# Convolution and two MLPs on one core: scaling by bank, another order of the first units, and two unused matmuls

## The chip, the cores and the metric

The kernel runs on one core of a Trainium2 chip. The time is that of the device for one execution in microseconds (us), the median of several runs. The core's engines are TensorE (PE, matmul), VectorE (DVE), ScalarE (ACT), GpSimd (POOL) and SyncE (SP, which issues the transfers here). They run side by side and wait for each other through semaphores.

## What is computed

8192 tokens of 192 features go through three steps in float32. The first is a causal convolution: each token sums itself and its six predecessors, with seven weights for each of 8 heads of 24 features, which are a softmax of `weight_gen`. The second is a gated MLP on the normalized rows, the third a plain one.

```python
w = np.exp(weight_gen - max); w = w / (sum(w) + 1e-9)      # 7 taps, 8 heads
x = einsum('bshk,bskhg->bshg', w, x_unf)                    # 8192 x 192
xn = x / np.sqrt(np.mean(x * x, -1) + 1e-6) * rms_g
g, val = xn @ w_gate, xn @ w_val                            # 192 x 1536
x = (g * sigmoid(g) * val) @ w_out                          # 1536 x 192
h = x @ w_in                                                # 192 x 2048
out = (h * sigmoid(1.702 * h)) @ w_out2                     # 2048 x 192
```

## The kernel before

The tokens go in 16 blocks of 512, four tiles of 128 each. A partition holds a run of 64 consecutive tokens. For a block the convolution is done with tokens on the partitions; then each row is scaled by its root mean square, the block is transposed on PE (`transpose_x`, L352), and it is split into a high part (`xh`, `xsh`, by ACT, L362) and a low part (`xl`, `xsl`, by DVE, L364), since a float32 product is made of three faster matmuls: high by high, low by high, high by low. `xh` and `xl` hold features 0 to 127, `xsh` and `xsl` the other 64 twice. So the copies of the scaling on ACT (L288) write features 128 to 191 a second time.

The blocks 0 and 1 are special. Block 0's taps are summed by DVE in two PSUM banks `ac` and `bc`, two tiles each: products into `xr` (L229), additions onto the banks (L256). Block 1's products are made by GpSimd and summed by PE through the identity (L247). ACT makes the square sums (L273), GpSimd the root: a multiply-add and a power (L278, L280). The result `ri` scales the rows.

The work of the MLPs is cut into units. A unit of the first MLP (`U1(b, m)`, 12 to a block) is the matmuls of one 128-wide piece of gate and value into two PSUM banks `pg` and `pv` (L381), then ACT's silu to `p` (L486), DVE's product (`second`, L490), ACT's cast to the high part `h` (L491) and DVE's subtraction to the low part `l` (`third`, L494). The matmuls with the down weights (`D1`, into the banks `a` and `b`) run two units later, within that unit's matmuls. There are four banks for `pg` and `pv`, so those of unit n are used again by unit n + 2. Every matmul uses half of the array's rows (64), two run side by side, and `matmuls` writes the two sequences as pairs; a bank goes from upper to lower rows through a GpSimd word (L396). A unit of the second MLP (`U2`) is alike, with two silu (L507, L508) and one subtraction for each half (L514).

The weights arrive as 64-bit words in 34 pieces, three at a time, and are turned into high and low parts on the way: ACT makes a first value (`x1`, L95), DVE cuts signs and masks (`x2`, L99 and L103), merges (`x3`, L107), cuts the high part (`x4`, L111), makes the low part (`x5`, L117), and ACT casts the high part (`x6`, L122). Pieces are called `w` (for `U1` and `U2`) and `o` (for `D1` and `D2`). While the pieces come in, in the first 120 us, they share DVE and ACT with the units of blocks 0 and 1.

The order on every engine is that of the program (`manual_schedule`). The list `units` sets the order of the units; `need` says at which unit each piece is due; `piece_steps` interleaves the steps of three pieces; `add_work`, `share` and `some` spread this and the later blocks' convolutions over the units, by costs in ns written in the code. The units before begin 0_0, 0_1, 1_0, 0_2, 1_1, 0_3, 1_2, 0_4, 0_5, 1_3, 0_6 (block and m), by this line:

```python
units += [(1, 0, t) for t in range(len([u for u in units if u[1] == 0]), min(M1, m + LAG + m // 3 + 1))]
units += [(1, 1, m)]
```

The softmax of blocks 2 and 3 needs one exponential on ACT (`ex_hook`, L188), placed four units after the start of that block's work; ACT loads a table before it and another one after it.

Of the kernel before, what the change touches and what calls it, by code (L numbers as in the profile page):

```python
# [9 lines left out]
F32 = mybir.dt.float32  # L10
F32R = mybir.dt.float32r
# [3 lines left out]
ALU = mybir.AluOpType  # L15
# [15 lines left out]
BLOCKS = [4] * 16  # L31
GROUPS = [(0, 1), (1, 2), (2, 4), (4, 7), (7, 10), (10, 13), (13, 16)]
AHEAD = 4
LAG = 1
LAG2 = 3
NST = 3
LOOK = 1
# [5 lines left out]
def gated_conv_mlp(ctx: ExitStack, tc: tile.TileContext, xp, wg, w1, wo1, w2, wo2, g, out):  # L43
# [113 lines left out]
    def softmax_load(gi):  # L157
        b0, b1 = GROUPS[gi]
        n = sum(BLOCKS[b0:b1])
        t = smw.tile([P, n * 56], F32, tag="wraw", name=f"wraw{gi}")  # L160
        nc.sync.dma_start(out=t, in_=wg[:, T0[b0] * 56:(T0[b0] + n) * 56])
        return t
# [55 lines left out]
    def conv_ops(b):  # L218

        T = BLOCKS[b]  # L220
        Q = T * HEADS
        x = xch[b]
        wn = wn_of[b]
        xr = att.tile([P, T, 2 * P], F32, tag="xr", name=f"xr{b}")
        prod = xr.rearrange("p t c -> p (t c)")[:, 0:Q * GRP]
        ops = []

        def mul(eng, k, dst, j0=0, j1=T):
            eng.tensor_tensor(  # L229
                out=dst.rearrange("p (q g) -> p q g", g=GRP),  # L230
                in0=x[:, (k + j0) * D:(k + j1) * D].rearrange("p (q g) -> p q g", g=GRP),
                in1=wn[:, j0 * HEADS:j1 * HEADS, k:k + 1].to_broadcast([P, (j1 - j0) * HEADS, GRP]), op=ALU.mult)
        cost = 1.04 * Q * GRP + 70
        if b < 2:
            S = T // 2
            sums_of = [pacc.tile([P, NM], F32, tag=f"{n}{b}", name=f"{n}c_{b}") for n in "ab"]
            acc_of = [sums_of[j // S][:, (j % S) * D:(j % S + 1) * D] for j in range(T)]
        else:
            acc = att.tile([P, T, D], F32, tag="acc", name=f"acc{b}")
            acc_of = [acc[:, j] for j in range(T)]  # L240
        if b == 1:
            def tap(k):
                for i, ps in enumerate(sums_of):
                    tag = (("yh", "yl"), ("ysh", "ysl"), ("yh0", "yl0"))[k % 3][i]
                    pr = ytp.tile([P, NM], F32R, tag=tag, name=f"pr{k}_{i}").bitcast(F32)[:, :S * D]
                    mul(nc.gpsimd, k, pr, i * S, (i + 1) * S)
                    nc.tensor.matmul(ps[:, :S * D], ident, pr, start=k == 0, stop=k == TAPS - 1)  # L247
            ops += [(cost, lambda k=k: tap(k)) for k in range(TAPS)]
        elif b == 0:
            n = S * D  # L250

            def tap(k):
                for i, ps in enumerate(sums_of):
                    mul(nc.vector, k, prod[:, i * n:(i + 1) * n] if k else ps[:, :n], i * S, (i + 1) * S)
                for i, ps in enumerate(sums_of if k else ()):
                    nc.vector.tensor_tensor(out=ps[:, :n], in0=ps[:, :n], in1=prod[:, i * n:(i + 1) * n], op=ALU.add)  # L256
            ops += [(cost, lambda k=k: tap(k)) for k in range(TAPS)]
        else:
            total = acc.rearrange("p t d -> p (t d)")

            def add():
                nc.vector.tensor_tensor(out=total, in0=total, in1=prod, op=ALU.add)  # L262
            for k in range(TAPS):
                ops.append((cost, lambda k=k: mul(nc.vector, k, prod if k else total)))
                if k:
                    ops.append((cost, add))
        ss = sml.tile([P, T], F32, tag="ss", name=f"ss{b}")
        ri = sml.tile([P, T], F32, tag="ri", name=f"ri{b}")

        def sq():  # L270
            room = xr if b != 1 else ytp.tile([P, NM], F32R, tag="yh", name="sq1").bitcast(F32).unsqueeze(1)
            for j in range(T):
                nc.scalar.activation(out=room[:, j if b != 1 else 0, 0:D], in_=acc_of[j], func=AF.Square,  # L273
                                     accum_out=ss[:, j:j + 1])
        ops.append((1500, sq))

        def root():
            nc.gpsimd.tensor_scalar(out=ss, in0=ss, scalar1=1.0 / D, scalar2=1e-6,  # L278
                                    op0=ALU.mult, op1=ALU.add)
            nc.gpsimd.tensor_tensor(out=ri, in0=ss, in1=half[:, :T], op=ALU.pow)  # L280
        ops.append((500, root))

        def sc(j):
            nc.vector.tensor_scalar_mul(out=xr[:, j, 0:D], in0=acc_of[j], scalar1=ri[:, j:j + 1])
            if b >= TURN:
                return
            i = (j + T // 2) % T if b < 2 else j
            nc.scalar.mul(out=xr[:, i, D:2 * P], in_=acc_of[i][:, P:D], mul=ri[:, i:i + 1])  # L288
        for j in range(T):
            ops.append((230, lambda j=j: sc(j)))  # L290
        xrow[b] = xr
        return ops

    def sums(b, nm):
# [296 lines left out]

    units = []
    for m in range(M1):
        units += [(1, 0, t) for t in range(len([u for u in units if u[1] == 0]), min(M1, m + LAG + m // 3 + 1))]
        units += [(1, 1, m)]
    for t in range(PAIRS + LAG2):
        units += [(2, 0, t)] if t < PAIRS else []
# [100 lines left out]
    with ExitStack() as order:  # L698
        order.enter_context(tc.manual_schedule())
        make_identity(nc, ident)  # L700
        nc.gpsimd.memset(half, -0.5)
        sm = {0: softmax_load(0), 1: softmax_load(1)}
        load_x(0, 1)
        load_pieces(0)
# [2 lines left out]
        def run(ops):  # L707
            for _, f in ops:
                f()
# [12 lines left out]
        conv, conv1 = conv_ops(0), conv_ops(1)  # L722
        run(conv[:TAPS])
        run(conv1[:TAPS])
        for r in line:
            r[0].pop(0)()
        for f in [c[TAPS + k][1] for c in (conv, conv1) for k in range(2)]:
            f()
        for f in line[0].pop(0) + line[0].pop(0) + line[1].pop(0):
            f()  # L730
        for f in line.popleft().pop(0):
            f()
        run(conv[TAPS + 2:])
        split = transpose_x(0)
        for f in line[0].pop(0):
            f()
# [1 line left out]
        for f in line[0].pop(0):  # L738
            f()
        line[0].append([])  # L740
        run(conv1[TAPS + 2:])
        sm[2] = softmax_load(2)
        for p, _ in need[1:]:
            add_work(0, max(0, p - LOOK), [(2150, piece_steps)])
        nxt = 2
        ex_hook = None
        start_at = pos[1, 1, 2]
# [1 line left out]
        for i, u in enumerate(units):  # L749
# [50 lines left out]
                downs.append(d)  # L800
                after += [f] if f else []
            second, third = (U1 if kind == 1 else U2)(b, m, lambda *ups: matmuls(ups, downs, kind == 2 and b < 2))
            todo = [share(k, i) / 2 for k in (0, 1)]
            if i == 0:
                split = transpose_x(1)
                split(dves=False)
                second()
                split(acts=False)
                third()
                some(todo)  # L810
                some(todo)
                for f in line[0].pop(0):
                    f()
            elif i < pos[2, 0, 0]:
                second()
                some(todo)
                some(todo)
                third()
            else:
                some(todo)  # L820
                second()
                some(todo)
                third()
# [60 lines left out]
```

## Time and profile before

| | before |
|---|---|
| median of 3 runs | 1236.8 us (1236.53 to 1237.01) |
| the profiled execution's own time | 1236.05 us |
| its span | 1234.1 us |
| its mean granted clock of PE | 0.998 |
| PE busy | 1214.5 us, 98% of the span |
| DVE busy | 772.0 us, 63% |
| ACT busy | 651.7 us, 53% |

The span is the profiler's, from the first instruction to the last; the execution's time is longer by what lies around it. PE is busy nearly all the time as a whole, but the first 120 us are of another kind than the rest: there the engines decode weights too, and the page's 40 slices show DVE at 80 to 90% for the first four slices and at some 60% later. The granted clock is a share of full speed, 2.4 GHz at 1.00 and 1.2 GHz at 0.50.

### The profile page before, as it was taken

The numbers are of one execution on the slowest core, as the hardware profiler recorded it, in microseconds if no ns is written. First come the engines' busy times: TensorE is split into PE (matmuls) and PEld (weight loads), VectorE is DVE, ScalarE is ACT, GpSimd is POOL, SyncE is SP. The second block draws the span as 40 slices with busy tenths as digits, with TensorE's granted clock in tenths as the row PEclk, the third lists the DMA queues.
The fourth block names the chain that finished last, engine by engine and source line by source line (L and its number), as shares of the span: only waits on it lengthen the run. The fifth ranks groups of instructions, "written<-read, shape, count | busy, mean of one in ns | idle before, by whom it ended". The sixth has DMA issues, their size and how long they took to land.

```text
span 1234.1 us, 26860 instructions
## 1 busy us (share of the span) xinstructions
PE 1214.5 (98%) x10324; PEld 1154.9 (94%) x10324; DVE 772.0 (63%) x1296; ACT 651.7 (53%) x1279; POOL 32.1 (3%) x53
## 2 busy tenths in 40 slices
PE   6999999999999999999999999999999999999998
PEld 3978998899899998999999999999999999899997
DVE  8999856567566574665747557475665746545432
ACT  4667754645546445454554545546454554544553
POOL 4000000000000000000000000000000000000000
PEclk9999999999999999999999999999999999999999
DMA  6856311001111001100011101001100011000000
GB/s 200 283 172 193 116 57 46 2 1 57 33 29 36 10 23 33 43 33 13 19 35 29 33 18 58 8 25 33 31 33 12 21 33 32 1 16 17 1 14 14
DMA packets 33856, 57.51 MB, mean 47 GB/s; under 512 B 7745, under 2 KB 19393, under 8 KB 33729
## 3 DMA queue, kind: packets, MB, share of 16 engines
q1 hardware_dynamic: 33728, 55.80, 14.5%
q8 instruction: 81, 1.33, 0.5%
q14 instruction: 47, 0.38, 0.1%
HBM read 43.71 MB, written 6.29 MB: 41 GB/s over the span
## 4 chain that ended last, share of the span: by engine, by line
PE 92%; DVE 6%; ACT 1%; issue 0%; DMA 0%; POOL 0%; SPq 0%; DVEq 0%; POOLq 0%
PE a L381 24%; PE ph L381 21%; PE pg L381 17%; PE b L381 16%; PE pv L381 14%; DVE p L490 1%; DVE l L494 1%; DVE xr L229 1%; DVE dec_a L107 1%; DVE w L117 0%; DVE dec_s L99 0%; DVE dec_s L111 0%; DVE l L514 0%; DVE acc L262 0%; DVE ac L256 0%
## 5 line engine op out<-in xcount | busy, mean ns | idle before, releaser
L381 PE MATMUL a<-h,o 64*128 64x512 f32 x1788 | 516.6, 391 | 0.0
L381 PEld LDWEIGHTS a<-h,o 64*128 64x128 f32 x1788 | 329.1, 185 | 6.7
L514 DVE TENSOR_TENSOR l<-p,h 128x512 fp32r<-128x512 f32 x256 | 176.1, 690 | 234.6 <-ACT p L508 233.6
L381 PE MATMUL b<-l,o 64*128 64x512 f32 x896 | 311.3, 393 | 0.3 <-DVE l L494 0.3
L381 PE MATMUL a<-l,o 64*128 64x512 f32 x894 | 310.4, 392 | 0.8 <-DVE l L514 0.7
L381 PE MATMUL b<-h,o 64*128 64x512 f32 x896 | 310.4, 392 | 0.0
L507 ACT ACTIVATE h<-ph 128x512 fp32r<-128x512 f32 x256 | 153.6, 600 | 206.5 <-PE ph L381 200.7
L381 PE MATMUL pg<-xh,w 64*128 64x512 f32 x768 | 240.6, 393 | 0.8 <-ACT w L122 0.7
L381 PE MATMUL pv<-xh,w 64*128 64x512 f32 x768 | 240.8, 393 | 0.3
L381 PE MATMUL ph<-yh,w 64*128 64x512 f32 x1024 | 237.5, 392 | 0.6 <-ACT yh L543 0.6
L491 ACT CAST h<-p 128x512 fp32r<-128x512 f32 x192 | 119.2, 621 | 181.6 <-DVE p L490 181.6
L486 ACT ACTIVATE p<-pg 128x512 f32<-128x512 f32 x192 | 114.4, 596 | 165.6 <-PE pg L381 148.6
L490 DVE TENSOR_TENSOR p<-p,pv 128x512 f32<-128x512 f32 x192 | 131.4, 684 | 106.4 <-PE a L381 83.4
L494 DVE TENSOR_TENSOR l<-p,h 128x512 fp32r<-128x512 f32 x192 | 132.3, 689 | 79.1 <-ACT h L491 78.9
L381 PEld LDWEIGHTS a<-l,o 64*128 64x128 f32 x894 | 165.0, 185 | 5.5 <-DVE l L514 2.1
L381 PEld LDWEIGHTS b<-l,o 64*128 64x128 f32 x896 | 165.4, 185 | 4.8 <-DVE l L494 1.6
L381 PEld LDWEIGHTS b<-h,o 64*128 64x128 f32 x896 | 164.6, 185 | 4.1 <-POOLq L396 0.3
L381 PEld LDWEIGHTS ph<-yh,w 64*128 64x128 f32 x1024 | 147.2, 184 | 10.5 <-ACT yh L543 1.0
L381 PE MATMUL ph<-yl,w 64*128 64x512 f32 x512 | 154.3, 392 | 0.2 <-DVE yl L546 0.2
L508 ACT ACTIVATE p<-ph 128x512 f32<-128x512 f32 x256 | 153.0, 598 | 0.5 <-DVE l L494 0.3
L381 PE MATMUL pv<-xl,w 64*128 64x512 f32 x384 | 150.8, 393 | 0.0
L381 PE MATMUL pg<-xl,w 64*128 64x512 f32 x384 | 150.2, 391 | 0.0
(117 smaller groups left out, 2096.3 us busy)
## 6 DMA issues: line engine op xcount, KB each, us to landing
x<-in_xp SPq DMA_DIRECT2D x15, 960.0 KB, 4.8
st<-in_w SPq DMA_DIRECT2D x20, 384.0 KB, 4.0
zt<-in_w SPq DMA_DIRECT2D x20, 384.0 KB, 3.5
st<-in_wo SPq DMA_DIRECT2D x14, 384.0 KB, 3.9
zt<-in_wo SPq DMA_DIRECT2D x14, 384.0 KB, 3.4
out_z<-za SPq DMA_DIRECT2D x16, 256.0 KB, 2.2
xl<-raw SPq DMA_DIRECT2D x176, 16.0 KB, 1.8
xsl<-raw SPq DMA_DIRECT2D x176, 16.0 KB, 1.8
```

What stands on the lines that cost most here:

```text
L107: nc.vector.scalar_tensor_tensor(out=ai, in0=ai, scalar=3, in1=t["s"], op0=ALU.logical_shift_left, op1=ALU.bitwise_or)
L229: eng.tensor_tensor(out=dst.rearrange("p (q g) -> p q g", g=GRP), in0=x[:, (k + j0) * D:(k + j1) * D].rearrange("p (q g) -> p q g", g=GRP) ...
L381: ins = nc.tensor.matmul(ps[:, :N], w[rows], x[rows, :N], start=start, stop=stop)
L486: nc.scalar.activation(out=p[:, :N], in_=pg[:, :N], func=AF.Silu)
L490: nc.vector.tensor_tensor(out=p[:, :N], in0=p[:, :N], in1=pv[:, :N], op=ALU.mult)
L491: nc.scalar.copy(h[:, :N], p[:, :N])
L494: nc.vector.tensor_tensor(out=l[:, :N], in0=p[:, :N], in1=h[:, :N].bitcast(F32), op=ALU.subtract)
L507: nc.scalar.activation(out=h[:, :N], in_=ps[j][:, :N], func=AF.Silu, scale=SIG)
L508: nc.scalar.activation(out=p[:, :N], in_=ps[j][:, :N], func=AF.Silu, scale=SIG)
L514: nc.vector.tensor_tensor(out=l[:, :N], in0=p[:, :N], in1=h[:, :N].bitcast(F32), op=ALU.subtract)
```

## The change

Block 0's last tap is done bank by bank: product and addition for bank a, then both for bank b. A dummy power stands on GpSimd at the program's start. Blocks 0 and 1 are scaled by one DVE operation for each bank (`rows`), with the root's value broadcast over the features, where four operations of one tile each stood before; ACT's four copies come together (`again`). Block 1's squares are cut in two halves around ACT's other work. After the taps PE gets two matmuls into a tile `heat` that nobody reads. A written table sets how many units of block 0 stand ahead of each unit of block 1, so that the order begins 0_0, 0_1, 1_0, 1_1, 0_2, 1_2, 0_3, 0_4, 1_3, 0_5. In unit 0 the second half of the first `o` piece's decode comes behind block 1's split, and `w_2` is due one unit later. The exponential stands behind the unit 1_3 in both orders, which is now the ninth unit and was the tenth.

```diff
-LAG = 1
+AHEAD_OF = (2, 2, 3, 5, 6, 7, 9, 10) + (M1,) * 4
...
+                steps = [(f, i) for f in ((product, add) if k else (product,)) for i in range(2)]
+                if k == TAPS - 1:
+                    steps = [steps[j] for j in (0, 2, 1, 3)]
+                for f, i in steps:
+                    f(i, sums_of[i])
...
+        if b < 2:
+            def rows():
+                for i, ps in enumerate(sums_of):
+                    nc.vector.tensor_tensor(
+                        out=xr[:, i * S:(i + 1) * S, 0:D], in0=ps[:, :S * D].rearrange("p (t d) -> p t d", d=D),
+                        in1=ri[:, i * S:(i + 1) * S].unsqueeze(2).to_broadcast([P, S, D]), op=ALU.mult)
+
+            def again():
+                for j in list(range(S, T)) + list(range(S)):
+                    nc.scalar.mul(out=xr[:, j, D:2 * P], in_=acc_of[j][:, P:D], mul=ri[:, j:j + 1])
...
-        units += [(1, 0, t) for t in range(len([u for u in units if u[1] == 0]), min(M1, m + LAG + m // 3 + 1))]
+        units += [(1, 0, t) for t in range(len([u for u in units if u[1] == 0]), AHEAD_OF[m])]
...
+        one = sml.tile([P, TM], F32, tag="ss", name="one")
+        nc.gpsimd.memset(one, 1.0)
+        nc.gpsimd.tensor_tensor(out=one, in0=one, in1=half, op=ALU.pow)
...
+        heat = pu.tile([P, NM], F32, tag="u", name="heat")
+        for _ in range(2):
+            nc.tensor.matmul(heat[:, :2 * D], ident, xch[0][:, 0:2 * D], start=True, stop=True)
...
-        run(conv[TAPS + 2:])
+        sq1a()
+        again0()
+        sq1b()
+        root1()
+        rows0()
...
-        for p, _ in need[1:]:
-            add_work(0, max(0, p - LOOK), [(2150, piece_steps)])
+        for k, (p, _) in enumerate(need[2:]):
+            add_work(0, p - LOOK if k else 2, [(2150, piece_steps)])
...
-            todo = [share(k, i) / 2 for k in (0, 1)]
+            todo = [share(k, i) / 2 for k in (0, 1)] if i > 3 else [1075, 0]
             if i == 0:
+                line.popleft()
                 split = transpose_x(1)
                 split(dves=False)
                 second()
+                marks, (x3, x4, x5), (n1, n2, n2m) = line[0].pop(0), line[0].pop(0), line[1].pop(0)
+                for f in marks + [x3]:
+                    f()
                 split(acts=False)
                 third()
-                some(todo)
-                some(todo)
-                for f in line[0].pop(0):
+                for f in [n1, n2, x4, n2m, x5] + line[0].pop(0):
                     f()
```

The first place is DVE at the scaling of block 0: `ac` and `bc` are its banks, `xr` its scaled rows, `ri` the root, `dec_a`, `dec_s` and `zt` a piece's intermediate values. Before:

```order
L103 TENSOR_SCALAR zt<-zt 128x384 [waits DMAHW7_49]
L284 TENSOR_SCALAR xr_156<-ac_157,ri_160 128x192 [waits Activation_49,Pool_49]
L284 TENSOR_SCALAR xr_156<-ac_157,ri_160 128x192
L284 TENSOR_SCALAR xr_156<-bc_158,ri_160 128x192 [waits Activation_49]
L284 TENSOR_SCALAR xr_156<-bc_158,ri_160 128x192
L107 SCALAR_TENSOR_TENSOR dec_a<-dec_a,dec_s 128x384 [waits DVE_49]
```

And now, on the same engine at the same place:

```order
L103 TENSOR_SCALAR zt<-zt 128x384 [waits DMAHW7_49]
L290 TENSOR_TENSOR xr_159<-ac_160,ri_163 128x2x192 [waits Activation_49,Pool_49]
L290 TENSOR_TENSOR xr_159<-bc_161,ri_163 128x2x192
L107 SCALAR_TENSOR_TENSOR dec_a<-dec_a,dec_s 128x384 [waits DVE_49]
L111 TENSOR_SCALAR dec_s<-dec_a 128x384 [waits DVE_49]
```

Four operations have become two. The first waits for ACT and GpSimd; in the built program the count of ACT for which it waits is that of the last of the four copies.

The second place is DVE behind the scaling of block 1, around unit 0's product `p_0_0` and low part `l_0_0`; `xl` and `xsl` are block 1's split, `o_130` (now `o_133`) the first `o` piece. Before:

```order
L284 TENSOR_SCALAR xr_161<-bc_163,ri_165 128x192
L99 TENSOR_SCALAR dec_s<-st 128x384 [waits DMAHW0_49]
L103 TENSOR_SCALAR zt<-zt 128x384 [waits DMAHW1_49]
L107 SCALAR_TENSOR_TENSOR dec_a<-dec_a,dec_s 128x384 [waits DVE_49]
L99 TENSOR_SCALAR dec_s<-st 128x384 [waits DMAHW3_49]
L111 TENSOR_SCALAR dec_s<-dec_a 128x384 [waits DVE_49]
L103 TENSOR_SCALAR zt<-zt 128x384 [waits DMAHW4_49]
L117 SCALAR_TENSOR_TENSOR o_130<-zt,dec_s 128x2x192 [waits DVE_49]
L490 TENSOR_TENSOR p_0_0_351<-p_0_0_351,pv_0_330 128x512 [waits Activation_49]
L364 SCALAR_TENSOR_TENSOR xl_356<-ax_359,gt,xh_355 128x512 [waits Activation_49]
L364 SCALAR_TENSOR_TENSOR xsl_358<-bx_360,gt,xsh_357 128x512 [waits Activation_49]
L494 TENSOR_TENSOR l_0_0_353<-p_0_0_351,h_0_0_352 128x512 [waits Activation_49]
```

And now, on DVE from the scaling of block 1:

```order
L290 TENSOR_TENSOR xr_164<-bc_166,ri_168 128x2x192
L505 TENSOR_TENSOR p_0_0_338<-p_0_0_338,pv_0_317 128x512 [waits Activation_49]
L99 TENSOR_SCALAR dec_s<-st 128x384 [waits DMAHW0_49]
L103 TENSOR_SCALAR zt<-zt 128x384 [waits DMAHW1_49]
L107 SCALAR_TENSOR_TENSOR dec_a<-dec_a,dec_s 128x384 [waits DVE_49]
L379 SCALAR_TENSOR_TENSOR xl_343<-ax_346,gt,xh_342 128x512 [waits Activation_49]
L379 SCALAR_TENSOR_TENSOR xsl_345<-bx_347,gt,xsh_344 128x512 [waits Activation_49]
L509 TENSOR_TENSOR l_0_0_340<-p_0_0_338,h_0_0_339 128x512 [waits Activation_49]
L99 TENSOR_SCALAR dec_s<-st 128x384 [waits DMAHW3_49]
L111 TENSOR_SCALAR dec_s<-dec_a 128x384 [waits DVE_49]
L103 TENSOR_SCALAR zt<-zt 128x384 [waits DMAHW4_49]
L117 SCALAR_TENSOR_TENSOR o_133<-zt,dec_s 128x2x192 [waits DVE_49]
```

The piece's decode stood whole in front of `p_0_0`; now all of it is behind that product, and its end behind the split and `l_0_0`.

The third place is ACT around the exponential (`wraw`, L188), with `h` and `p` of the units by block and m, or by m alone. Before:

```order
L491 CAST h_1_3_878<-p_1_3_877 128x512
L188 ACT_TABLE_LOAD
L188 ACTIVATE wraw_311<-wraw_311 128x448
L486 ACT_TABLE_LOAD
L486 ACTIVATE p_0_6_925<-pg_6_889 128x512
L491 CAST h_0_6_926<-p_0_6_925 128x512
L122 CAST w_7_657<-dec_a 128x384
```

And now, on ACT at the exponential's new place:

```order
L506 CAST h_1_3_809<-p_1_3_808 128x512
L122 CAST w_6_589<-dec_a 128x384
L95 ACTIVATE dec_a<-st 128x384
L188 ACT_TABLE_LOAD
L188 ACTIVATE wraw_314<-wraw_314 128x448
L501 ACT_TABLE_LOAD
L501 ACTIVATE p_0_5_870<-pg_5_834 128x512
L506 CAST h_0_5_871<-p_0_5_870 128x512
L122 CAST o_649<-dec_a 128x2x128
```

A cast of a weight piece and the first step of another one now stand between `h` of unit 1_3 and the table load, and the next silu is that of 0_5.

## Rows read from the trace of the kernel before

**Rows 1.** Page, part 1: busy time, share of the span, instructions.

```profile
PE 1214.5 (98%) x10324; PEld 1154.9 (94%) x10324; DVE 772.0 (63%) x1296; ACT 651.7 (53%) x1279; POOL 32.1 (3%) x53
```

**Rows 2.** Windows: length, busy PE, PEld, DVE, ACT, POOL, clock, DMA, GB/s.

```profile
25.00:26.00 1.00, 1.00 (x6) 0.67 (x8) 1.00 (x3) 1.00 (x3) 0.00 (x0) 0.50 0.25 79
...
75.00:110.00 35.00, 33.95 (x285) 29.23 (x285) 34.24 (x73) 21.81 (x46) 0.00 (x0) 1.00 0.63 202
```

**Rows 3.** Timeline of PE, 19 to 34 us: start, duration, instruction, [idle before].

```profile
19.53 0.81 PE L247 MATMUL bc<-pr,ident 128*128 128x384 f32 x2
23.48 0.66 PE L352 MATMUL ax<-ident,xr 128*128 128x128 f32 x4 [3.13 <-ACT xr L288]
...
27.21 0.59 PE L381 MATMUL pg<-xsl,w 64*128 64x512 f32 x1
...
27.91 0.49 PE L381 MATMUL pv<-xh,w 64*128 64x512 f32 x1
...
31.19 0.39 PE L381 MATMUL pg<-xsl,w 64*128 64x512 f32 x1
...
31.70 0.49 PE L381 MATMUL pv<-xh,w 64*128 64x512 f32 x1
...
33.97 0.39 PE L381 MATMUL b<-h,o 64*128 64x512 f32 x1
```

**Rows 4.** Timeline of DVE, 18 to 30 us.

```profile
18.20 0.56 DVE L256 TENSOR_TENSOR ac<-ac,xr 128x384 f32<-128x384 f32 x1
18.66 0.56 DVE L256 TENSOR_TENSOR bc<-bc,xr 128x384 f32<-128x384 f32 x1
...
19.66 0.55 DVE L107 SCALAR_TENSOR_TENSOR dec_a<-dec_a,dec_s 128x384 int32<-128x384 int32 x1
20.25 0.36 DVE L111 TENSOR_SCALAR dec_s<-dec_a 128x384 int32<-128x384 int32 x1
...
22.82 0.74 DVE L284 TENSOR_SCALAR xr<-bc,ri 128x192 f32<-128x192 f32 x2
...
25.59 0.74 DVE L364 SCALAR_TENSOR_TENSOR xsl<-bx,gt,xsh 128x512 fp32r<-128x512 f32 x1
...
29.38 0.54 DVE L117 SCALAR_TENSOR_TENSOR o<-zt,dec_s 128x384 fp32r<-128x384 int32 x1
29.85 0.67 DVE L490 TENSOR_TENSOR p<-p,pv 128x512 f32<-128x512 f32 x1
```

**Rows 5.** Timeline of ACT, 22 to 30 us.

```profile
22.26 0.52 ACT L288 ACTIVATE xr<-bc,ri 128x64 f32<-128x64 f32 x2
...
24.17 0.69 ACT L362 ACTIVATE xh<-ax,gt 128x512 fp32r<-128x512 f32 x1 [0.75 <-PE ax L352]
...
29.00 0.60 ACT L486 ACTIVATE p<-pg 128x512 f32<-128x512 f32 x1 [1.01 <-PE pg L381]
```

**Rows 6.** Timeline of POOL: the powers of blocks 0 and 1.

```profile
20.74 1.35 POOL L280 TENSOR_TENSOR ri<-ss,half 128x4 f32<-128x4 f32 x1
...
22.45 1.01 POOL L280 TENSOR_TENSOR ri<-ss,half 128x4 f32<-128x4 f32 x1
```

**Rows 7.** Timeline of DVE, ACT and PE behind the exponential.

```profile
64.14 0.69 DVE L490 TENSOR_TENSOR p<-p,pv 128x512 f32<-128x512 f32 x1 [3.11 <-ACT p L486]
...
65.39 0.51 ACT L122 CAST w<-dec_a 128x384 fp32r<-128x384 f32 x1
65.80 0.57 ACT L95 ACTIVATE dec_a<-st 128x384 f32<-128x384 f32 x1
...
65.95 0.49 PE L381 MATMUL pg<-xh,w 64*128 64x512 f32 x1 [0.69 <-ACT w L122]
...
66.28 0.57 ACT L486 ACTIVATE p<-pg 128x512 f32<-128x512 f32 x1
```

**Rows 8.** Timeline of DVE and PE where the second MLP begins.

```profile
114.17 1.28 DVE L514 TENSOR_TENSOR l<-p,h 128x512 fp32r<-128x512 f32 x2
...
114.90 0.49 PE L381 MATMUL a<-l,o 64*128 64x512 f32 x1 [0.66 <-DVE l L514]
```

More of the change, by code (lines that the diff above doesn't have):

```diff
@@ L252, in tap, with product, add @@
             def tap(k):
-                for i, ps in enumerate(sums_of):
+                def product(i, ps):
                     mul(nc.vector, k, prod[:, i * n:(i + 1) * n] if k else ps[:, :n], i * S, (i + 1) * S)
-                for i, ps in enumerate(sums_of if k else ()):
+                def add(i, ps):
                     nc.vector.tensor_tensor(out=ps[:, :n], in0=ps[:, :n], in1=prod[:, i * n:(i + 1) * n], op=ALU.add)
+                steps = [(f, i) for f in ((product, add) if k else (product,)) for i in range(2)]
[3 more added lines that the diff above has]
+                    f(i, sums_of[i])
             ops += [(cost, lambda k=k: tap(k)) for k in range(TAPS)]
@@ L268, in conv_ops, with sq @@
         ri = sml.tile([P, T], F32, tag="ri", name=f"ri{b}")
-        def sq():
-            room = xr if b != 1 else ytp.tile([P, NM], F32R, tag="yh", name="sq1").bitcast(F32).unsqueeze(1)
-            for j in range(T):
+        def sq(js=range(T)):
+            room = xr if b != 1 else ytp.tile([P, NM], F32R, tag="yh", name=f"sq1_{js[0]}").bitcast(F32).unsqueeze(1)
+            for j in js:
                 nc.scalar.activation(out=room[:, j if b != 1 else 0, 0:D], in_=acc_of[j], func=AF.Square,
                                      accum_out=ss[:, j:j + 1])
-        ops.append((1500, sq))
         def root():
@@ L280, in root @@
             nc.gpsimd.tensor_tensor(out=ri, in0=ss, in1=half[:, :T], op=ALU.pow)
+        xrow[b] = xr
+        if b < 2:
[7 more added lines that the diff above has]
+                    nc.scalar.mul(out=xr[:, j, D:2 * P], in_=acc_of[j][:, P:D], mul=ri[:, j:j + 1])
+            return ops + [(0, f) for f in (lambda: sq(range(S)), lambda: sq(range(S, T)), root, again, rows)]
+        ops.append((1500, sq))
         ops.append((500, root))
@@ L284, in sc @@
             nc.vector.tensor_scalar_mul(out=xr[:, j, 0:D], in0=acc_of[j], scalar1=ri[:, j:j + 1])
[L285 to L288, printed above, removed]
+            if b < TURN:
+                nc.scalar.mul(out=xr[:, j, D:2 * P], in_=acc_of[j][:, P:D], mul=ri[:, j:j + 1])
         for j in range(T):
             ops.append((230, lambda j=j: sc(j)))
-        xrow[b] = xr
         return ops
@@ L724, in gated_conv_mlp @@
         run(conv1[:TAPS])
+        heat = pu.tile([P, NM], F32, tag="u", name="heat")
+        for _ in range(2):
+            nc.tensor.matmul(heat[:, :2 * D], ident, xch[0][:, 0:2 * D], start=True, stop=True)
         for r in line:
             r[0].pop(0)()
-        for f in [c[TAPS + k][1] for c in (conv, conv1) for k in range(2)]:
-            f()
+        sq0a, sq0b, root0, again0, rows0 = [f for _, f in conv[TAPS:]]
+        sq1a, sq1b, root1, again1, rows1 = [f for _, f in conv1[TAPS:]]
+        sq0a()
+        sq0b()
+        root0()
         for f in line[0].pop(0) + line[0].pop(0) + line[1].pop(0):
@@ L740, in gated_conv_mlp @@
         line[0].append([])
-        run(conv1[TAPS + 2:])
+        again1()
+        rows1()
         sm[2] = softmax_load(2)
-        for p, _ in need[1:]:
-            add_work(0, max(0, p - LOOK), [(2150, piece_steps)])
+        for k, (p, _) in enumerate(need[2:]):
+            add_work(0, p - LOOK if k else 2, [(2150, piece_steps)])
         nxt = 2
```

## The prediction

> **What bounds the kernel now.** The page's first part comes first: PE is busy for 98% of the span, DVE for 63% [rows 1]. The work of PE hardly changes (two small matmuls), so the time can move only where PE waits or runs slowly. The windows by stage show where that is [rows 2]: in 25 to 26 us the granted clock is 0.50, that is 1.2 GHz and not 2.4, with PE busy all the time; in 75 to 110 us PE lacks 1.05 of 35 us while DVE is busy 34.24. So three places count: the start up to some 30 us, the unit at which ScalarE does the exponential (64 to 68 us), and the begin of the second MLP (114 us). Behind them PE has no wait that this change touches. All times below are microseconds.
>
> The timeline gives the start as a chain. Block 0's last addition on DVE ends at 18.66 + 0.56 = 19.22 [rows 4]; ScalarE's squares and GpSimd's first operation lie between it and the power, which runs from 20.74 to 22.09 [rows 6]; the DVE scaling runs to 22.82 + 0.74 = 23.56 [rows 4]; the transposes start at 23.48 after 3.13 without PE work [rows 3]; ScalarE splits at 24.17 [rows 5]; the sixth pair of unit 0 waits until 27.21 and its second half starts at 27.91 [rows 3]. In this stretch the clock is low, and the same step from pair six to the second half takes 27.91 - 27.21 = 0.70, against 31.70 - 31.19 = 0.51 in unit 1 at full clock [rows 3].
>
> **The change part by part.**
>
> *Last tap by banks.* Product a, add a, product b, add b now depend on one another in turn. Independent DVE operations on 384 elements start 0.46 apart (18.20, 18.66), dependent ones 0.59 (19.66, 20.25) [rows 4]. Two such dependences: 2 x 0.13 = +0.26 on the last addition. Its gain, that bank a is ready earlier, is small, since the second square writes where product b is read and so waits for the last addition as before. The page "VectorE: DVE Perf Modes" of the Trainium skill, section "The DRAIN you can't avoid", says that the next operation starts only when the pipe is empty and that a semaphore adds nothing; by it this edit would cost 0, and the sum would be 0.26 less. The rows differ, and they decide: +0.25.
>
> *Power warmed up.* The first power takes 1.35, the second 1.01 [rows 6]. If what the first has in excess is a first-use cost, the early dummy power takes 0.34 off: bounds 0 and -0.34. I take -0.34, since both rows have the same shape. The root is ready at 22.09 + 0.25 - 0.34 = 22.0.
>
> *Scaling by banks.* In the new order the four copies of ScalarE come together, and the first DVE operation waits for the last of them. A pair of copies is 0.52 long [rows 5], so four end about 4 x 0.26 = 1.04 after 22.05, at 23.09. The two DVE operations of 2x192 are not in the trace; the nearest row is the addition on 384 elements out of PSUM, 0.56 [rows 4], and the lower bound is two operations at 0.46 apart. From 23.12 they end at 24.15, that is 24.15 - 23.56 = +0.59 for all that DVE does next. The first pair of transposes needs only the first operation and starts at 23.71 against 23.48; the third and fourth (0.66 for four [rows 3]) need the second, so ScalarE's split comes at about 24.15 + 0.33 + 0.15 = 24.63, against 24.17 [rows 5]. Without the wait on the copies they would end at 23.1: that is the bound below, -0.5.
>
> *Two unused matmuls.* One 128x384 matmul is up to 0.81 in the trace [rows 3]. PE's work so ends at 20.34 + 1.3 = 21.6, and the idle time before the transposes is 2.1 and not 3.13. They cost PE nothing, since nothing else is ready there. What they may bring is the clock. Before, the clock falls just after that idle time, with the transposes already running, and is 0.50 in the first pairs of unit 0 [rows 2]. I take it that it now stays up; the other case is a rival below.
>
> *Unit 0.* DVE does the rest of a piece and then the two splits, without an idle moment; the second split ended at 25.59 + 0.74 = 26.33 [rows 4] and now at 26.92. Pair six needs it and starts at about 27.08 (some 0.15 for the semaphore and the pair's start), 0.13 earlier than at the low clock. With 0.51 in place of 0.70 the second half starts at 27.59, and unit 1 with all behind it 0.32 to 0.34 earlier. I take **-0.34** up to there. Block 1's scaling, held by its own four copies, ends some 0.1 before its transposes then want it.
>
> *First down piece (o) behind block 1's split.* Before, o was decoded by 29.38 + 0.54 = 29.92, ahead of the product p of unit 0 at 29.85 [rows 4]. Now DVE waits for ScalarE's silu, whose row ends at 29.00 + 0.60 = 29.60 [rows 5], now 29.26, and then does p, mask, shift, merge, two splits, l, two masks, shift and o's last: durations 0.67 + 0.35 + 0.35 + 0.55 + 0.74 + 0.74 + 0.67 + 0.36 + 0.36 + 0.36 + 0.54 = 5.69, less some 0.08 of overlap at each of ten steps = 4.89 (p, the split, merge, mask and o's last from [rows 4]). It ends at 29.28 + 4.89 = 34.17. Unit 2's first matmul with o stood at 33.97 [rows 3] and would stand at 33.63. PE waits 0.54 and about 0.1 for its restart (0.49 for a pair after a wait, 0.39 otherwise [rows 3]): **+0.65**. What DVE then does is in step with before, one piece behind, and w_2 is needed one unit later, so I cost that at nothing; if DVE stays late, a piece's five steps, 0.35 x 3 + 0.55 + 0.54 less overlaps = 1.75, are the price.
>
> *Exponential one unit earlier.* Its place in ScalarE's order is now behind the cast of a piece of weights and the next piece's first step. By starts these take 65.80 - 65.39 = 0.41 and 66.28 - 65.80 = 0.48 [rows 7]. ScalarE has two table loads around the exponential, so the silu behind it comes up to 0.89 later against the units. DVE already idled 3.11 for that silu [rows 7], so no cover is left on it, and the unit two later needs the bank that p releases. Before, the cost at this place was 0.69 of PE idle, put down to a cast of weights [rows 7], and some 0.3 for a late l. Bounds: -0.7 (that cast is not late any more, and nothing takes its place) and +0.89. I take **+0.65**, near the upper end because the idle DVE row is the one it is nearest to.
>
> *Second MLP's begin.* DVE now does l_0_0, a piece (1.75) and a conv product before l_0_1, where before both l stood together, 114.17 to 115.45, and PE waited 0.66 for them [rows 8]. l_0_1 ends up to 0.85 later; PE needs it after the matmuls with l_0_0, so 0 to +0.85. I take **+0.4**.
>
> **Sum.** -0.34 + 0.65 + 0.65 + 0.4 = +1.4. The profiled execution took 1236.05 (span 1234.1 and 1.95 around it), so 1237.4; the median of the runs, 1236.8, lies 0.75 above it, so **1238.2**.
>
> **The rivals.** A difference of 0.2%, 2.5, is about what a measurement of this kernel can tell from none: 1234.3 and 1239.3 are the bounds.
>
> *B, the gains carry through.* The clock stays, and the exponential in its new place takes away the 0.69 of idle and the 0.3 behind it rather than adding. For it: that idle was put down to a cast that is now placed ahead. Against: two more instructions ahead of the table loads. -0.34 + 0.65 - 1.0 = -0.7, so 1236.1; with o early enough -1.3, 1235.5; if the scaling is not held either, another -1.0, 1234.5. Some of this is needed to come out measurably faster.
>
> *C, the clock falls again.* For it: the low clock began with transposes running [rows 2], and 2.1 idle remains. Then nothing of unit 0 is faster, and the +0.46 of the split on ScalarE (24.17 to 24.63) is carried on: 0.46 + 0.34 = 0.8 more than the sum, 1239.0; with the upper bound at the second MLP's begin 1239.5. By the page "TensorE: Matmul & The Clock Gate" of the Trainium skill, Part 4, transposes do not count as PE work for the clock in the same way; by that rule the two matmuls alone would have to bridge to unit 0, and this is the case that it speaks for. The trace agrees as far as it goes: the clock was low from the transposes on.
>
> *D, slower: DVE stays one piece behind.* Place: the units up to the exponential, where DVE is busy without a gap. If o's last step is late and each following piece comes late too, PE waits for a piece once more by up to 1.75: 1.4 + 1.75 = +3.15, 1239.9. It decides from the point where a piece's last step lies more than one unit behind where it lay before. Against: the new order needs each piece one unit later.
>
> **How the numbers follow.** The forecast 0.45, B 0.27, C 0.18, D 0.10. Measurably faster is about half of B: 0.14. Measurably slower is D and some of C: 0.16. The same: 0.70. The range from 1235.0 to 1240.0 leaves out the far ends of B and of D, about one in ten on each side.
>
> **What the profile would show.** The clock window of 25 to 26 tells C from the rest. The second scaling operation's end shows the wait on the copies (24.15 or 23.1); the last tap's spacings show 0.59 or 0.46; the power 1.01 or 1.35. An idle PE of about 0.6 ahead of a matmul with o in unit 2, released by DVE, shows the late piece; its absence makes B. Around the exponential the idle times of PE, summed, should be some 1.6; under B they are under 0.5. What makes the forecast wrong most easily is a change in the long DVE-bound stretch from 75 to 110, which I take to be the same in both.

## The result

The changed kernel takes 1244.18 us (median of 4 runs, 1242.53 to 1244.84), before 1236.66 (4 runs). The ratio is 1.0061, 95% interval 1.0048 to 1.0073: 7.5 us slower, where 1238.2 was forecast and 1240.0 was the upper end. Its profiled execution took 1242.53 us with a span of 1240.7, 6.6 longer than the span before.

Page, part 1 of the changed kernel; beside [rows 1], PE is busy for 2.6 us more and idle for 4.0 more:

```profile
PE 1217.1 (98%) x10328; PEld 1139.0 (92%) x10328; DVE 771.8 (62%) x1292; ACT 652.0 (53%) x1279; POOL 33.9 (3%) x55
```

The start in the timeline of PE, changed kernel (start, duration, instruction, idle before and what ended it):

```profile
19.50 1.45 PE L745 MATMUL heat<-x,ident 128*128 128x384 f32 x4
23.89 0.90 PE L367 MATMUL ax<-ident,xr 128*128 128x128 f32 x4 [2.94 <-DVE xr L290]
...
27.28 0.39 PE L396 MATMUL pg<-xsl,w 64*128 64x512 f32 x1
...
27.79 0.50 PE L396 MATMUL pv<-xh,w 64*128 64x512 f32 x1
...
34.53 0.47 PE L396 MATMUL b<-h,o 64*128 64x512 f32 x1 [0.39 <-DVE o L117]
```

Beside [rows 3] the second half of unit 0 begins at 27.79 and not at 27.91, and the first matmul that needs the low part of `o` at 34.53 and not at 33.97 (the one ahead of it, with the high part, did not wait). DVE and GpSimd around it, against [rows 4, 6]:

```profile
18.22 0.55 DVE L229 TENSOR_TENSOR xr<-x,wn 128x384 f32<-128x384 f32 x1
18.80 0.57 DVE L257 TENSOR_TENSOR bc<-bc,xr 128x384 f32<-128x384 f32 x1
...
23.28 0.56 DVE L290 TENSOR_TENSOR xr<-ac,ri 128x384 f32<-128x384 f32 x1 [1.39 <-ACT xr L296]
23.76 0.55 DVE L290 TENSOR_TENSOR xr<-bc,ri 128x384 f32<-128x384 f32 x1
...
33.84 0.55 DVE L117 SCALAR_TENSOR_TENSOR o<-zt,dec_s 128x384 fp32r<-128x384 int32 x1
```

```profile
1.46 1.03 POOL L719 TENSOR_TENSOR one<-one,half 128x4 f32<-128x4 f32 x1
...
20.89 1.33 POOL L285 TENSOR_TENSOR ri<-ss,half 128x4 f32<-128x4 f32 x1
...
24.30 1.33 POOL L285 TENSOR_TENSOR ri<-ss,half 128x4 f32<-128x4 f32 x1
```

The scaling is held by ScalarE's copies, as the order said, and the power is not shorter (the first row of GpSimd is the dummy power). In this execution the granted clock is full in the window where it was 0.50 before [rows 2]:

```profile
25.00:26.00 1.00, 0.66 (x7) 0.30 (x4) 0.96 (x3) 1.00 (x3) 0.63 (x1) 1.00 0.23 92
```

Behind the exponential, timeline of PE: the 0.69 idle for a cast [rows 7] is gone, and two waits for DVE stand there, the greater for a low part:

```profile
63.48 0.49 PE L396 MATMUL pv<-xh,w 64*128 64x512 f32 x1 [0.23 <-DVE p L505]
...
66.35 0.50 PE L396 MATMUL b<-l,o 64*128 64x512 f32 x1 [0.98 <-DVE l L509]
```

And the second MLP's first units, timeline of PE:

```profile
118.67 0.49 PE L396 MATMUL a<-l,o 64*128 64x512 f32 x1 [1.91 <-DVE l L529]
...
124.89 0.49 PE L396 MATMUL a<-l,o 64*128 64x512 f32 x1 [1.06 <-DVE l L529]
...
139.26 0.50 PE L396 MATMUL a<-l,o 64*128 64x512 f32 x1 [0.46 <-DVE l L529]
```

One such wait, of 0.66, stood there before [rows 8]. DVE ahead of the first of them, end of a piece, a convolution product and then the late `l`:

```profile
116.59 0.55 DVE L117 SCALAR_TENSOR_TENSOR w<-zt,dec_s 128x384 fp32r<-128x384 int32 x1
117.06 0.95 DVE L229 TENSOR_TENSOR xr<-x,wraw 128x768 f32<-128x768 f32 x1
117.93 0.68 DVE L529 TENSOR_TENSOR l<-p,h 128x512 fp32r<-128x512 f32 x1
```

Laid side by side matmul by matmul, the changed execution is 0.14 us ahead at 31 us, 0.6 behind from 35 us, 0.7 behind at 61, 1.8 behind at 82, 2.3 at 112, 3.2 at 118, 4.5 at 121, 5.5 at 148 and 6.0 at 192. (These are starts of the n-th matmul of the MLPs in either timeline; the places are times of the kernel before.) So half of the loss, 3.2, falls between 112 and 148 us, where the prediction had put 0.4.

### The profile page after: what moved, and what is told of

Same layout as the page of the kernel before. It is cut to its first block, busy times and chain, and to the rows that moved or that the text cites. A ratio compares the mean times of both kernels' runs of the same rounds, so it can differ in the third digit from the quotient of the medians.

```text
span 1240.7 us, 26866 instructions
## 1 busy us (share of the span) xinstructions
PE 1217.1 (98%) x10328; PEld 1139.0 (92%) x10328; DVE 771.8 (62%) x1292; ACT 652.0 (53%) x1279; POOL 33.9 (3%) x55
## 4 chain that ended last, share of the span: by engine, by line
PE 93%; DVE 5%; issue 1%; ACT 0%; DMA 0%; POOL 0%; DVEq 0%; POOLq 0%
PE a L396 25%; PE ph L396 21%; PE b L396 16%; PE pv L396 16%; PE pg L396 15%; DVE xr L229 1%; DVE l L529 0%; DVE dec_a L107 0%; DVE l L509 0%; DVE p L505 0%; DVE acc L268 0%; DVE w L117 0%; DVE dec_s L111 0%; DVE dec_s L99 0%; DVE ac L257 0%
```

## The experiments

Times are medians against the kernel before on the same chip (1235.81, 1236.10, 1236.19 and 1236.41 in the four sets); a signed time is the difference from it. In the edits `after` means the changed kernel and `before` the old one. The expectations call their explanations by letters. P: the new order puts side work between the two `l` of a unit of the second MLP, and the exponential a unit earlier. S: the late start is carried on to the second MLP. Q: the pieces come late there, whatever their place. P2 and S2 are told where they stand.

**Which part: the order of units alone, or all but it.**

```diff
 before, run b_table
-min(M1, m + LAG + m // 3 + 1)
+AHEAD_OF[m]
 after, run a_lagorder
-AHEAD_OF = (2, 2, 3, 5, 6, 7, 9, 10) + (M1,) * 4
+AHEAD_OF = tuple(min(M1, m + m // 3 + 2) for m in range(M1))
```

> The kernel before with only the written order of units. Theory P: +1.3 us at the exponential, +0.4 around 93 to 100 us, +3.3 us in the second MLP's first units, so 1241.7 us. Rival S: the old start stays, so 1236.7 us within 1 us.

Measured: 1241.06, +5.2, ratio 1.0044 (1.0027 to 1.0060). The table alone makes most of the loss, with the old start. Waits of PE for DVE's `l` (L514 before, in the table's run the same line) between 111 and 145 us, before and with the table: in total, times, longest.

```profile
PE a L381 <- DVE l L514: 0.7, 1, 0.7
```

```profile
PE a L381 <- DVE l L514: 3.5, 3, 1.9
```

> The changed kernel with the old order of units; the start, the heat matmuls and the decode in unit 0 stay changed. Theory P (the written order moves the decode pieces between the two l of a unit of the second MLP, and puts the exponential one unit earlier): both losses vanish, +0.5 of the late o piece stays, 1237.2 us, within 1 us. Rival S (the late start of DVE's decode is carried to the second MLP): 1242 to 1244 us.

Measured: 1239.02, +3.2, ratio 1.0024 (1.0014 to 1.0033). The loss of the second MLP went, that of the start was greater than expected: in its profile the clock was low from 23.1 to 30.0 us, and between 33 and 42 us some 1.5 more are lost, where PE waits for the low part of `o` (0.4) with DVE a piece late and the old order asking for each piece one unit earlier. Theory P holds for the place, its sum for the start does not.

**Is it the piece between the two `l`?** In a unit of the second MLP, `some(todo)` writes decode and convolution steps once ahead of the first `l` and once between the two; a credit decides which of the two gets the piece. On DVE the order is piece, `l`, `l` before, and `l`, piece, product, `l` with the table.

```diff
 after, run a_p2first
-some(todo); second(); some(todo); third()
+some(todo); some(todo); second(); third()
 before, run b_p2split
+if i == pos[2, 0, 0]: credit[0] -= 1075
```

> The changed kernel with the decode and convolution work of a unit of the second MLP written ahead of both l. Theory P: the 3.3 us of the second MLP's first units vanish, the exponential's stay, 1240.9 us. Rival S: 1244 us within 1 us.

Measured: 1241.15, +5.3, ratio 1.0041 (1.0026 to 1.0056). It wins some 2 us on the changed kernel's 7.5, less than expected: the convolution's product now stands ahead of both `l`, so the first one is late (PE idle 1.53 at 118.38), and in its profile the clock is 0.50 at 120 us.

> The kernel before, but with half a piece taken off the credit at the first unit of the second MLP, so that each piece comes between the two l there. Theory P: 1236.7 + 3.3 = 1240 us. Rival S: 1236.7 us within 1 us.

Measured: 1237.82, +2.0, ratio 1.0013 (1.0004 to 1.0023). Right in sign, and smaller. The place is not quite the same: here the piece alone stands between the two `l` of the first unit (112.88 and 115.23 on DVE) and the product behind both, and PE waits 1.6 in all, in four waits; the old order also brings DVE to these units earlier.

**Late pieces, or the place?** One run brings the pieces forward and leaves one between the two `l`; others put the piece ahead of both and the convolution behind both.

```diff
 before with the table, run bt_p2early9
-add_work(0, max(0, p - LOOK), ...)
+add_work(0, max(0, p - LOOK - (p >= pos[1, 1, 9])), ...)
 before with the table, run bt_convlast; before, run b_convlast
-some(todo); second(); some(todo); third()
+some([2 * todo[0], 0]); second(); third(); some([0, 2 * todo[1]])
 after, run a_look2
-LOOK = 1
+LOOK = 2
```

> The kernel before with the written order of units, and from the tenth unit of block 1 on every piece due one unit earlier; in the second MLP a piece still stands between the two l of each unit, but it is the next one. Theory P: the loss stays, 4 to 5 us above before. Rival Q (the pieces were late): the loss there goes, 1.5 to 2 us above before.

Measured: 1240.75, +4.6, ratio 1.0043 (1.0028 to 1.0058).

> The kernel before with the written order of units, and in the units of the second MLP the piece's steps ahead of both l, the convolution's behind them. Theory P (a piece or a product between the two l of a unit is what PE waits for): of the 5.2 us that the written order alone cost, the 3.2 us at 112 to 140 us go, 1.5 to 2 us above before are left. Rival Q (pieces come late there, whatever stands between): 4 to 5 us above before.

Measured: 1239.22, +3.0, ratio 1.0026 (1.0016 to 1.0036). PE's waits between 111 and 145 us, first with earlier pieces, then with the other place:

```profile
PE a L381 <- DVE l L514: 3.4, 3, 1.9
```

```profile
PE a L381 <- DVE l L514: 0.7, 1, 0.7
```

That decides for the place: with pieces one earlier the wait is as before them, with the place changed it is that of the old kernel. In its timeline bt_convlast is 0.9 behind before at 112 us and 0.3 at 202; most of its 3.0 us arise later (2.8 behind at 300), where the edit changed the later blocks' units too.

> The kernel before, its order of units kept, and in the units of the second MLP the convolution's steps behind both l. If PE's wait of 0.66 at 114.9 us and small ones behind it come from DVE's place for l, up to 1 us less than before, 1235 us. If the convolution then is late for its own block, 1 us more.

Measured: 1237.39, +1.2, ratio 1.0011 (1.0002 to 1.0021). By the starts of its matmuls it is 0.35 us ahead of before at 202 us (the 1.25 in the expectation of b_cl2 below is too much) and 1.2 behind at 300: in the later blocks the convolution behind both `l` is not free.

> The changed kernel with every piece due one unit earlier (LOOK = 2), which brings the pieces of the second MLP's first units from between the two l ahead of both. Theory P2 (the loss there comes from pieces rationed too late): the 3.3 us at 115 to 140 us shrink to 1 or less, some 4.5 us above before. Rival: the first units now lack DVE time for l, so that what is won there is lost ahead, 7 us above before.

Measured: 1242.79, +6.7, ratio 1.0057 (1.0040 to 1.0074). The rival's way: the loss from 112 us on shrinks to 0.4 (5.8 behind at 110, 6.2 at 151), and 2.0 more are lost by 50 us, where PE waits 1.0 for a `p` and 0.5 for an `l` behind early pieces.

**The edit for blocks 0 and 1 alone, which leaves the later blocks as they are.**

```diff
 before, run b_cl2; after, run a_cl2; after with old order and unit 0, run os_cl2
+if b < 2: some([2 * todo[0], 0]); second(); third(); some([0, 2 * todo[1]])
 before with the table and this, run bt_cl2ex
-ex_at = i + 4 if gi == 2
+ex_at = i + 5 if gi == 2
```

> The changed kernel with the same edit for blocks 0 and 1 alone. Theory P (a piece or product between the two l of a unit): of its 7.5 us some 4 go, 3.5 us above before is left (start and o piece 1.5, exponential 1.3, 93 to 100 us 0.4). Rival Q (late pieces): 6.5 us or more.

Measured: 1238.67, +2.3, ratio 1.0016 (1.0007 to 1.0025): 5.2 of the 7.5 us go. Laid beside the changed kernel's timeline, 3.6 of them go between 112 and 148 us and 0.7 more by 202. DVE in that run; the piece is ahead of both `l`, the product behind:

```profile
117.49 0.57 DVE L117 SCALAR_TENSOR_TENSOR w<-zt,dec_s 128x384 fp32r<-128x384 int32 x1
117.96 1.31 DVE L529 TENSOR_TENSOR l<-p,h 128x512 fp32r<-128x512 f32 x2
119.16 0.98 DVE L229 TENSOR_TENSOR xr<-x,wraw 128x768 f32<-128x768 f32 x1
```

The windows from 111 to 145 us, changed kernel and then this run: length, busy PE, PEld, DVE, ACT, POOL, clock, DMA, GB/s.

```profile
111.00:145.00 34.00, 30.56 (x253) 26.76 (x251) 28.08 (x58) 22.63 (x48) 0.00 (x0) 1.00 0.54 172
```

```profile
111.00:145.00 34.00, 33.01 (x275) 29.34 (x277) 32.57 (x68) 25.33 (x56) 0.00 (x0) 1.00 0.63 190
```

DVE was not the engine with too much to do: where PE waits for `l`, PE gives DVE nothing to do next, and DVE idles 5.9 us of the 34 (1.4 in the other order).

> The kernel before with the convolution's steps behind both l in the units of the second MLP of blocks 0 and 1 alone (later blocks as before). The same edit for all blocks was 1.25 us ahead at 202 us and lost it behind. If that loss is the later blocks' alone, 1.2 us below before, 1235 us. If moving the convolution at all is late for block 2, within 0.5 us of before.

Measured: 1236.01, -0.4, ratio 0.9994 (0.9985 to 1.0003): as before within the measurement, though 0.5 us ahead in the timeline at 202 us. This was the version that might have beaten both kernels; it beats the changed one.

> The kernel before with the written order of units, the edit of the second MLP's units of blocks 0 and 1, and the exponential one unit later, so that it is behind the tenth unit as before. If its place behind a cast and a first decode step is what costs 0.7 us at 66 us, that offset against before goes, and the kernel is 0.5 to 1.2 us below before. If the order of units itself costs it, the offset of 0.7 us at 66 us stays, and it is at before.

Measured: 1237.64, +1.2, ratio 1.0010 (1.0000 to 1.0019). With the exponential behind the tenth unit again, PE's waits at 60 to 72 us are 1.0 for an `l` and 0.2 for a `p`, the same as in the changed kernel between 60 and 70. So its unit is not the cause; by the matmuls' starts the place costs 0.4 here and 0.7 in b_table. But the run did not take away what the expectation names, for in this order a cast and a first decode step stand ahead of the table load at the later unit too:

```profile
61.07 0.62 ACT L491 CAST h<-p 128x512 fp32r<-128x512 f32 x1 [0.97 <-DVE p L490]
61.60 0.60 ACT L122 CAST o<-dec_a 128x256 fp32r<-128x256 f32 x2
62.11 0.55 ACT L95 ACTIVATE dec_a<-st 128x384 f32<-128x384 f32 x1
62.68 1.28 ACT L188 ACT_TABLE_LOAD   x1
```

So this run does not test that cause. An earlier one does: bt_p2early9 has the new order, the two instructions and a silu just as late, and its timeline loses nothing at this place (0.3 behind before at 61 us and at 83). ScalarE there, from `h` of unit 1_3 to the next silu, and DVE behind it:

```profile
57.04 0.62 ACT L491 CAST h<-p 128x512 fp32r<-128x512 f32 x1 [1.21 <-DVE p L490]
...
61.85 0.60 ACT L486 ACTIVATE p<-pg 128x512 f32<-128x512 f32 x1
```

```profile
62.48 0.69 DVE L490 TENSOR_TENSOR p<-p,pv 128x512 f32<-128x512 f32 x1 [3.13 <-ACT p L486]
63.09 0.61 DVE L191 TENSOR_REDUCE mx<-wraw 128x64 f32<-128x448 f32 x1
63.85 0.69 DVE L494 TENSOR_TENSOR l<-p,h 128x512 fp32r<-128x512 f32 x1 [0.16 <-ACT h L491]
```

In the changed kernel, as in b_table and here, a piece stands on DVE between that `p` and its `l`, ahead of the softmax's reduction:

```profile
62.73 0.69 DVE L505 TENSOR_TENSOR p<-p,pv 128x512 f32<-128x512 f32 x1 [3.02 <-ACT p L501]
...
65.08 0.61 DVE L191 TENSOR_REDUCE mx<-wraw 128x64 f32<-128x448 f32 x1
65.61 0.68 DVE L509 TENSOR_TENSOR l<-p,h 128x512 fp32r<-128x512 f32 x1
```

PE's wait of 1.0 for `l` goes with that piece, and not with the late silu alone. (The kernel before has a piece there too, its `l` starting at 67.02, but PE had already waited 0.69 for the cast just ahead [rows 7].)

**The start and the first `o` piece.**

```diff
 after, run a_oldsched: old order of units, old unit 0, old credits
 after, run a_oldu0: old unit 0, old credits
 after, run a_rowsfirst
-sq1a(); again0(); sq1b(); root1(); rows0()
+rows0(); sq1a(); again0(); sq1b(); root1()
-again1(); rows1()
+rows1(); again1()
 after, run a_noheat
-for _ in range(2):
+for _ in range(0):
```

> The changed kernel with the old order of units, the old place of the first o piece in unit 0 and the old credits; only the start itself (last tap, power, scaling, squares, heat) stays changed. Theory P2 (the order of units alone costs some 4.6 us, the o piece behind block 1's split the next 1 to 2 us): within 1 us of before. Rival S2 (the start itself costs, because the first scaling waits for ScalarE's four copies and DVE's idle time there is carried on): 2 to 3 us above before.

Measured: 1236.73, +0.6, ratio 1.0005 (0.9996 to 1.0015). The new start alone is neutral.

> The new start (last tap, power, scaling, squares, heat) with the old order, the old unit 0 and the edit of the second MLP's units of blocks 0 and 1. If the parts add, 0.6 - 1.2 = 0.6 us below before, and so 0.6 us above the run with the old start: the new start buys nothing.

Measured: 1236.30, -0.1, ratio 0.9998 (0.9989 to 1.0007); it says the same.

> The changed kernel with the first o piece and the credits of the first units as before; the written order and the new start stay. If the parts add, it is the new start (+0.6) and the written order (+5.2), 5.8 us above before, and the o piece's new place with the credits is worth the 1.7 us that are left to the changed kernel. If the o piece's new place is what pays for the order, it is above the changed kernel, 8 us or more.

Measured: 1242.86, +6.7, ratio 1.0058 (1.0043 to 1.0073). PE has no wait for `o` between 31 and 37 us here, and the total is 0.8 below the changed kernel's, so the piece's place and the credits are worth about that; the intervals overlap.

> The changed kernel with both scalings by bank written ahead of ScalarE's four copies, so that they wait for the root alone. If the hold is on the path, unit 0's second half comes 1.0 us earlier and the kernel takes 1.0 us less than the changed one, some 6.5 us above before. If DVE's later pieces set the end anyway, no change within 0.5 us.

Measured: 1244.41, +8.3, ratio 1.0070 (1.0055 to 1.0085). No gain, and the hold is turned round rather than gone: the first scaling starts 1.05 earlier, at 22.23, but ScalarE's copies now wait for the scaling and PE's transposes for the copies. ScalarE, then PE:

```profile
23.35 0.52 ACT L296 ACTIVATE xr<-bc,ri 128x64 f32<-128x64 f32 x2 [1.69 <-DVE xr L290]
```

```profile
24.33 0.48 PE L367 MATMUL ax<-ident,xr 128*128 128x128 f32 x1 [3.23 <-ACT xr L296]
```

In its profile the clock is also 0.50 from 24 to 29 us. The question what the kernel would take without any such hold stays open.

> The changed kernel without the two unused matmuls. If they keep the clock up, the clock falls here in every execution and costs 0.7 to 1 us, some 8.3 us above before. If they do nothing reliable, as the low clock in two runs that had them suggests, it is the changed kernel's time within 0.5 us, and the granted clock at 24 to 27 us is 0.50.

Measured: 1243.73, +7.6, ratio 1.0065 (1.0050 to 1.0080): no different from the changed kernel. Its windows show the clock falling before any transpose runs (PE's first one starts at 24.02, after 4.24 idle):

```profile
22.00:23.00 1.00, 0.00 (x0) 0.00 (x0) 0.01 (x1) 0.62 (x4) 0.34 (x1) 0.78 0.88 191
23.00:24.00 1.00, 0.00 (x0) 0.00 (x0) 0.59 (x2) 0.97 (x6) 0.00 (x0) 0.50 0.75 258
...
28.00:29.00 1.00, 0.89 (x7) 0.17 (x3) 0.91 (x2) 0.00 (x0) 0.00 (x0) 0.50 0.95 364
```

## Why the prediction was wrong

**The step that failed is the term for the second MLP's begin, +0.4.** The order showed there, on DVE, that a piece and a product come between `l_0_0` and `l_0_1`, and the prediction priced it as one lateness of 0 to 0.85. At that one place it was the upper bound: the offset grows by 0.87 there (2.29 to 3.16). What failed is that it was counted once. The same `some(todo)` puts work between two `l` again in units behind it, and these cost 1.33 (at 124.89) and 0.87 (at 139.26). PE waits three times, 3.4 in all where 0.7 stood, and the offset grows by 3.2 between 112 and 148 us. By a_cl2 against the changed kernel the place is worth 5.2 us of the medians (0.4 of which the same edit gives the old kernel too), 4.4 of them in the timelines between 112 and 202 us. The table sets it off without touching these units: it shifts when pieces are rationed, and so in which half of a unit the credit runs out; taking half a piece off the credit in the old order (b_p2split) gives the like.

**The exponential, +0.65.** Right in kind (the cast's wait goes, waits for DVE take its place), mis-sized: the offset grows by 1.1 between 61 and 82 us in the changed kernel, and by 0.7 in b_table, near the forecast. The lateness given is there in full: from the start of `h` of unit 1_3 to that of the next silu ScalarE takes 4.70 (57.40 to 62.10) where it took 3.82 (59.69 to 63.51), 0.88 more against the 0.89 of the prediction. ScalarE before, then changed:

```profile
59.69 0.62 ACT L491 CAST h<-p 128x512 fp32r<-128x512 f32 x1 [0.98 <-DVE p L490]
...
63.51 0.60 ACT L486 ACTIVATE p<-pg 128x512 f32<-128x512 f32 x1
```

```profile
57.40 0.62 ACT L506 CAST h<-p 128x512 fp32r<-128x512 f32 x1 [1.23 <-DVE p L505]
...
62.10 0.60 ACT L501 ACTIVATE p<-pg 128x512 f32<-128x512 f32 x1
```

But it does not make the cost by itself: bt_p2early9 takes 4.81 for the same and loses nothing here. The greater wait comes with a piece between `p` and `l` on DVE, the same kind of place as in the second MLP, and the prediction did not look at DVE there. This rests on one run, in which other pieces have moved too.

**The first `o` piece, +0.65,** was right: some 0.7 by the matmuls' starts, its last step ending at 33.84 + 0.55 = 34.39 against a forecast of 34.17.

**The start, -0.34.** The last tap's dependence is there: 0.58 between a product and its addition (18.22 to 18.80), 0.46 without dependence [rows 4]. The Trainium skill's "VectorE: DVE Perf Modes", section "The DRAIN you can't avoid", would have it free; the rows decide again. The hold by ScalarE's copies came as forecast (23.28), the two scaling operations took 1.03 (23.28 to 24.31), as taken. The warm power was wrong: 1.33 both times, while the dummy one, the first of all, took 1.03; so the 0.34 was no cost of first use. The root is ready at 22.22 and not at 22.0, and all that follows comes 0.2 later than forecast, down to the second half of unit 0 (27.79, forecast 27.59). The prediction also misread pair six before: it did not wait for the second split, which ended at 26.33, but came at 27.21, 0.43 behind pair five, the distance of all pairs there from the second on, at the low clock. Pair five before, then two rows of the changed kernel, where PE waits ahead of earlier pairs, for the first splits:

```profile
26.78 0.63 PE L381 MATMUL pg<-xsh,w 64*128 64x512 f32 x1
```

```profile
25.58 0.49 PE L396 MATMUL pg<-xh,w 64*128 64x512 f32 x1 [0.34 <-ACT xh L377]
...
26.47 0.50 PE L396 MATMUL pg<-xl,w 64*128 64x512 f32 x1 [0.17 <-DVE xl L379]
```

In sum the profiled execution gained 0.14, where 0.34 was forecast.

**The clock, rival C.** I had taken it to stay up. It did in the changed kernel's profile, but the other three of its runs have a mean granted clock of 0.995 or 0.996 against 0.999, and are 1.1 to 2.3 us longer. Of the nine profiled executions with the two matmuls, eight had a low clock at the start, and the run without them took as long. So C was the usual case; by the matmuls' starts these eight are 0.5 to 1.7 behind before at 31 us, where the one without a fall is 0.14 ahead. The reason I gave for it from the Trainium skill ("TensorE: Matmul & The Clock Gate", Part 4, transposes do not count as PE work in the same way) is neither shown nor needed: without the two matmuls the clock fell while PE did nothing, before the transposes; in some runs with them too (0.57 from 23 to 24 us in a_lagorder, first transpose at 23.96); and with them it once stayed full through the same transposes.

What the prediction did not think of is a second fall, in the second MLP. In four profiles (a_p2first, a_rowsfirst, a_noheat, a_oldu0) the clock is low once more, somewhere between 118.8 and 125.7 us, and it falls within 1.4 us of the end of PE's wait of 1.5 to 1.9 for `l`. In a_oldu0, PE and then its window:

```profile
118.83 0.79 PE L396 MATMUL a<-l,o 64*128 64x512 f32 x1 [1.92 <-DVE l L529]
```

```profile
119.00:120.00 1.00, 1.00 (x6) 0.81 (x8) 0.00 (x0) 0.00 (x0) 0.00 (x0) 0.50 0.95 307
```

The three of these that have the changed order of DVE there (all but a_p2first) lose 3.9 to 4.8 between 112 and 148 us, where the changed kernel's profile, with the same wait and no fall, loses 3.2. So such a wait can cost more than its own length. Whether the changed kernel's three longer executions had such a fall is not known; only the fourth was profiled.

**Rival D** named the right engine and the wrong place: up to the exponential DVE keeps up, apart from the first `o`.

Of 7.5 us, then: some 4 to 5 are the place of pieces in the second MLP's first units, about 0.7 the place of the first `o`, and the rest, some 2, the waits behind the exponential (1.1 in the changed kernel's timeline) and the clock. These last are not separated beyond that.

## What to carry to other kernels

When a table changes the order of units, read the new order not only at the units that move but wherever a rationing rule fills in side work: a shift by half a piece can put work between two results that the critical engine takes at once, in several of the units that follow. A term found at one unit of a loop has to be priced once for each turn in which it comes back. And a kernel whose engines each have slack can still lose when a side job stands ahead of the one instruction that another engine waits for: compare a_cl2 with the changed kernel, where only the place was changed.

## What was not expected of the hardware

The low clock at the start is not the same in every execution of a kernel: among the profiles with the two unused matmuls it lasted from none (25 to 26 us at 1.00) to 6.8 us, with the idle time ahead of it nearly alike (2.94 in the one without a fall, 2.89 in one where it was low from 23.1 to 30.0). Nor does a wait of 1.9 us in the second MLP always have the same outcome: the clock stayed full behind it in the changed kernel's profile and was low in three others. A power on four columns took 1.35 and 1.01 before, and 1.03 (the dummy) and twice 1.33 after, so 0.3 of it depends on something that these runs do not show.
